# A gated feed-forward layer on one core: order of loads and stores between its first two stages

## The chip, the cores and the metric

The kernel runs on one core of one Trainium2 chip. The metric is device time in microseconds (us), from the start of the program to its end. The core has five engines with queues of their own, and 16 DMA engines that they share: TensorE (PE, matmuls; its weight loads are listed as PEld), VectorE (DVE), ScalarE (ACT), GpSimd (POOL) and SyncE (SP), which here issues the DMA transfers and nothing else.

## The reference

```python
def _gelu(x):
    return jax.nn.gelu(x, approximate=True)
...
B, S, Dm, Df = 1, 2048, 1024, 3584
...
def reference(x, w_gate, w_up, w_down):
    g = jnp.einsum("bsd,df->bsf", x, w_gate)
    u = jnp.einsum("bsd,df->bsf", x, w_up)
    h = _gelu(g) * u
    return jnp.einsum("bsf,fd->bsd", h, w_down)
```

All arrays are bfloat16.

## The kernel before

**Passes and stages.** The 2048 rows of x are taken in two passes (`ip`) of 1024 rows, each as two column blocks of 512. A pass has two stages. The first makes h: 14 *units* of 256 columns of `w_gate` and `w_up` each. The second, `down`, multiplies h with `w_down`, whose 28 blocks of 128 rows are taken as 14 *blocks* `j` in two halves `kh`.

**Fewer products.** Both stages use a seven-product scheme of 2 by 2 blocks instead of eight products. That needs sums of blocks, which are made in 32 bits: `s1` to `s4` of weights (mostly GpSimd, `pool`), `t1` to `t4` of x (DVE), and copies `sa`, `tb` (ACT). For the units 4 to 13 of the first pass (`pair0`, two units at a time) one of the seven products is itself split once more; its sums are `r1` to `r4`, and x's are kept in the tile `forms`. What the second pass needs again of it goes to device memory (`pd`).

**Differences of w_down.** The down stage's products use three differences of blocks of `w_down` for each `j`. They are made once, in the first pass, and stored to device memory (`td`) for both passes. For most blocks ACT and DVE make them between the products (`keep_part`, line 578 on). Blocks 12, 13 and 11 are made by GpSimd at the end of the first stage (`keep_whole`, three subtractions each). `BIGS` lists 1, 4, 12, 13, 11: blocks whose raw weights lie in a large tile of the pool `w`; `fetch_wd` loads them.

**The end of the first stage.** `last_of_0` is the last pair (units 12 and 13) of the first pass. In the order of its calls on SP: `hooks("made", 10)` stores the differences of block 10 and then loads four raw down tiles ahead (`fetch12(0)` to `fetch12(3)`; one such tile feeds two blocks j of one half kh); `hooks("wholes", 0)` loads block 11, has GpSimd make blocks 12, 13 and 11, and stores 12; `hooks("pd", 13)` stores one part of `pd`; `hooks("home", 13)` is `bring_home`, eight copies that gather parts of h, kept elsewhere until then, into the tile `hL`, which takes the place of `forms`; `hooks("pd", 12)`; and `hooks("wholes", 1)`, close to the end, stores 13.

**The down stage.** `down` runs over steps. Steps 0 to 13 multiply the first half's raw tiles with h, steps 14 to 27 the second half's: 4 matmuls each, so 8 for each raw tile. From step 28 on the second product uses the second differences (`q12`, reloaded from `td` by `load12`) and sums of h (`s12`, made by DVE in `make12`). From step 31 the first differences follow. From step 45 come `q73` and at last `q4` with `sa`. What is issued at a step is an agenda: `need12` fetches raw tile n at step 2n - 8 unless it was fetched ahead; `load12(j)` runs at step `AT12[j]`, where j = 0, 2, 4 load two blocks at once into a tile of the pool `w` (1 MB) and j = 6, 7 go to the pool `m`; `make12(j)` at `AT12S[j]`; `fetch73` and `make73` at `AT73[j] - 3` and `AT73[j]`. `more(step)` holds what the first pass does for the second beside that: the store of block 11 at step 2, x's next transposing loads from step 24, the next weights at step 50 and their sums at step 58.

**Order.** `manual_schedule` fixes the order of SP, DVE, GpSimd and PE as the code calls them (ACT's too in the first stage). So an SP transfer that must wait holds back all transfers behind it. The pools hand out buffers in the order in which they were given back: `k` has 36 slots of 2 KB per partition (raw tiles, x's sums, `u2`, `p5`, `g`, `q` and others), `s` has 13, `w` three, `m` two. A transfer into a slot waits until the slot's last readers are done.

The names in the profile: `raw<-in_w_down_dram` from L658 are the raw tiles of `fetch12`, from L641 those of `fetch73`; `w<-in_w_down_dram` and `raw<-in_w_down_dram` from L575 are `fetch_wd`; `td<-m` from L601 and L603 are the stores of differences; L950 is `pd`; L350 to L355 are `bring_home`; L613, L618 and L624 are `load12`; L634 is `load4`; L788 is x's transposing load; L144 loads `w_gate` and `w_up`. All matmuls of the stages go through L134, DVE's sums through L110, GpSimd's through L113.

Of the kernel before, what the change touches and what calls it, by code (L numbers as in the profile page):

```python
# [10 lines left out]
def kernel(  # L11
# [52 lines left out]
    BIGS = (1, 4, 12, 13, 11)  # L64
    LAG = 3
    BIG12 = (0, 2, 4)
    AT12 = [6, 6, 10, 10, 14, 14, 16, 18, 20, 22, 27, 29, 31, 33]
    AT12S = [2 * j + (j > 8) for j in range(NJ)]
    AT73 = [30 + 2 * j if j < 8 else 46 + j - 8 for j in range(NJ)]

# [391 lines left out]
    def last_of_0(a, roles, sa, sb, q, t, A, B, p5a, u2b, u2r, hooks):  # L462
        F, C, K, E = roles
        b = a + 1
        dve(F[1], F[1], p5a[1], SUB)
        part(E, q["r1"], T1, True)
        p5r = [snap(E[i], "p5", A[i]) for i in range(2)]
        part(K, q["r3"], T3, False)
        for i in range(2):
            dve(A[i], K[i], p5r[i], ADD)  # L470
        times(2 * a + 1, 0, gelu(F[0]), F[1])
        sb.make("sa")
        hooks("wholes", 0)
        part(E, q["r4"], TB, False)
        hooks("pd", b)
        part(K, [x[:, H:] for x in sb["s1"]], T4, False)
        hooks("home", b)
        for i in range(2):
            dve(B[i], E[i], u2r[i], ADD)
        hooks("pd", a)  # L480
        full(C, sb["s3"], t["t3"])
        p5b = [snap(K[i], "p5") for i in range(2)]
        full(K, sb["s4"], t["tb"])
        g, up = add(C, p5b)
        g = gelu(g)
        times(2 * b + 1, 1, g, up)
        full(C, sb["sa"], t["t4"])
        hooks("wholes", 1)
        hadd(K, u2b, 2 * b, 1)
        squared(C, p5b, 2 * b + 1)  # L490
        return roles
# [72 lines left out]

    def fetch_wd(js):
        for j in js:
            if j not in BIGS:
                wraw[j] = [slot([P, Dm], bf16, "raw") for _ in range(2)]
            else:
                n = BIGS.index(j) % 2  # L570
                if n == 0:
                    big = wpool.tile([P, 4, Dm], bf16, name="w")
                wraw[j] = [big[:, 2 * n + kh] for kh in range(2)]
            for kh in range(2):
                nc.sync.dma_start(out=wraw[j][kh], in_=wdn[:, kh, j, :])  # L575
# [303 lines left out]
    def upgraded(u):  # L879
        return FIRST <= u <= LAST  # L880
# [30 lines left out]
    for ip in range(NPASS):  # L911
        with tc.manual_schedule(engines={ENG.Activation}):
            if ip == 0:
                ws = {1: w, 2: ahead}
                late = lambda: add(cc, nxt["p1"])
            else:
                raw_of(0, F)()
                raw_of(1, C)()
            for u in range(1 if ip == 0 else 0, NU):
                if upgraded(u):  # L920
                    if u % 2:
                        continue
                    if u == FIRST:
                        S = {u: s, u + 1: sums_s(W(u + 1), pool)}
                    if (ip, u) == (0, FIRST):
                        fetch_wd(MID.values())
                        for n in range(4):
                            for c in range(2):
                                away[NH + n, c] = lambda n=n, c=c: staged(n, c)
                        away[NH + 4, 0] = lambda: hx  # L930

                    def hooks(what, n):
                        if what == "w":
                            if n < NU:
                                W(n)
                            if (ip, n) == (0, NU):
                                fetch_wd(BIGS[2:4])
                            if ip == 0 and n - 3 in JS:
                                fetch_wd(JS[n - 3][1:])
                            if ip == 0 and n - 2 == NH // 2 + 1:  # L940
                                send_out()
                            if ip == 0 and n - 3 == NH // 2 + 1:
                                move_on()
                            if ip and n <= LAST:
                                fetch_p5(n)
                        if what == "home" and n == LAST:
                            bring_home()
                        if what == "pd":
                            k = 0 if n % 2 else KH
                            nc.sync.dma_start(  # L950
                                out=pd[:, n - FIRST].rearrange("p i n -> p (i n)"),
                                in_=flat(xT[1][:, k : k + KH]),
                            )
                        if what == "made":
                            store_made(n)
                            if n == JS[LAST - 1][0]:
                                for m in range(4):
                                    fetch12(m)
                                    ahead12.add(m)
                        if what == "wholes" and n == 0:  # L960
                            fetch_wd(BIGS[4:])
                            for j in BIGS[2:]:
                                keep_whole(j)
                            store_made(BIGS[2])
                        if what == "wholes" and n == 1:
                            store_made(BIGS[3])
                        if what == "fetch":
                            fetch_wd(JS[n + 2][:1])

                    roles = F, C, K, E  # L970
                    if ip == 0:
                        F, C, K, E = pair0(u, roles, S, t, JS[u], hooks)
                    else:
                        F, C, K, E = pair1(u, roles, S, t, hooks)
                    continue
                first = (ip, u) == (0, 1)

                def prepare():
                    if first:
                        pool_behind(t["t4"][-1])  # L980
                    if ip == 0 and u in (2, 3):
                        lo_part(u - 2, 3, K)
                    if u + 1 < NU:
                        nxt["s"] = make_s(W(u + 1), pool, nxt.get("s"))
                    if (ip, u) == (0, FIRST - 2):
                        fetch_wd(JS[FIRST][:1])

                def keep(part, ps):
                    if ip == 0 and u in (2, 3):
                        for n in ((0, 1), (), (2,))[part]:  # L990
                            lo_part(u - 2, n, ps)

                def aside(part):
                    if first and part < 0:
                        rest_of_0(part + 2)
                    if part == 0 and u + 2 < NU:
                        W(u + 2)
                        if ip and upgraded(u + 2):
                            fetch_p5(u + 2)
                        if (ip, u) == (0, 1):  # L1000
                            load_lo()
                    if part == 0 and "t4" not in t:
                        t.make("t4")

                def ahead_of_p4():
                    if u % 2 and u + 1 < NU:
                        raw_of(u + 1, F)()
                        nxt["c11"] = raw_of(u + 2, C)

                def behind_p4():  # L1010
                    if "c11" in nxt:
                        nxt.pop("c11")()

                if u % 2 and not first:
                    E, K, C = C, E, K
                banks = (E, K, C) if u % 2 else (F, K, E)
                unit(
                    u, banks, s, t, late if first else None, prepare, aside, keep,
                    ahead_of_p4, behind_p4,
                )  # L1020
                s = nxt.pop("s", None)
# [4 lines left out]
        def more(step):  # L1026
            if last:
                return
            if step == 2:
                store_made(BIGS[4])  # L1030
            if step == 0:
                xT[:] = new_x()
            if step >= 24 and step % 2 == 0 and step // 2 - 12 < len(moves):
                c, ko = moves[step // 2 - 12]
                transposing(xT, c, ko, (2 * (ip + 1) + c) * N)
            if step == 50:
                ws.clear()
                ws.update({n: load_w(n) for n in range(2)})
            if step == 58:
                got["s"] = make_s(ws[0], dve)  # L1040
            if step == 62:
                got["t"] = make_t(xT)
# [34 lines left out]
```

## Time and profile before

| | us |
|---|---|
| median of three runs | 548.55 (546.86 to 548.73) |
| the profiled execution | 547.19 |
| its span | 545.4 |
| PE busy | 531.4 (97%) |
| DVE busy | 369.1 (68%) |
| ACT busy | 281.6 (52%) |
| POOL busy | 270.2 (50%) |
| first stage, first pass, to | 197.6 |
| down stage, first pass, to about | 296.6 |

The profiled execution lasts 1.8 us longer than its span, which runs from the first to the last instruction. The page gives first the busy time of each engine, then the span in 40 slices of 13.6 us with each engine's busy tenths, the granted clock of PE and the DMA engines' share; then the chain of work that ended last, by engine; then groups of instructions with their mean time and what ended the idle time before them. In a timeline, a line is the start and duration of a group of instructions of one kind, and in brackets the idle time before it and what ended that. SPq is SP's queue; its lines show how long SP took to issue a transfer, not how long that took. A line of a table of stretches gives for each engine its busy time and the number of instructions, then granted clock, DMA share and GB/s. In the whole execution the core moved 107.71 MB, 197 GB/s on average.

### The profile page before, as it was taken

The page shows a single profiled execution, that of the slowest core. Times are in us where ns is not written, and L with a number is a line of the kernel's source. Part 1 is how long each engine was busy: PE and PEld are TensorE (multiplying, and loading weights), DVE is VectorE, ACT ScalarE, POOL GpSimd, SP SyncE. Part 2 cuts the span into 40 slices and gives each one's busy share as a digit, 9 for nine tenths or more (in the row PEclk, how much of TensorE's full clock was granted, in tenths as well). Part 3 has the DMA queues.
Part 4 walks back from the last instruction along what each step waited for, and adds up shares of the span by engine and source line. Part 5 has one row for each costly group of instructions (what it writes and reads, how often), then busy time and mean ns, then how long its engine had stood idle before and what let it go on. Part 6 is the DMA issues. An engine that isn't in the chain of part 4 may idle for free.

```text
span 545.4 us, 7557 instructions
## 1 busy us (share of the span) xinstructions
PE 531.4 (97%) x2389; PEld 376.7 (69%) x2389; DVE 369.1 (68%) x573; ACT 281.6 (52%) x508; POOL 270.2 (50%) x258
## 2 busy tenths in 40 slices
PE   8999999999999994999999999999999999999997
PEld 4568686868686861378887768676686675488885
DVE  2989678787777794556877654665765859875830
ACT  3567686968686720104354555656566662104351
POOL 1089958879897940000003868896679740000000
PEclk9999999999999997999999999999999999999999
DMA  9795227676676879997894835233834439655571
GB/s 250 169 241 151 78 94 270 197 270 214 210 239 235 271 258 339 390 304 201 228 299 170 217 106 143 82 103 87 231 103 131 115 101 361 251 174 159 169 242 48
DMA packets 118407, 107.71 MB, mean 197 GB/s; under 512 B 22112, under 2 KB 98656, under 8 KB 118368
## 3 DMA queue, kind: packets, MB, share of 16 engines
q1 hardware_dynamic: 118368, 107.24, 64.7%
q8 instruction: 19, 0.31, 0.2%
q14 instruction: 20, 0.16, 0.1%
HBM read 80.22 MB, written 20.97 MB: 186 GB/s over the span
## 4 chain that ended last, share of the span: by engine, by line
PE 91%; DMA 4%; SPq 2%; DVE 2%; issue 0%; ACT 0%; DVEq 0%; ACTq 0%
PE bank L134 91%; DMA raw<-in_w_down_dram 2%; DMA w<-td 1%; DVE q L110 1%; DMA w<-in_w_up_dram 1%; SPq L601 1%; SPq L658 1%; DVE hL L110 0%; SPq L775 0%; DVE bank L110 0%; SPq L950 0%; SPq L618 0%; ACT g L202 0%; DVE sum L110 0%; ACT st L747 0%
## 5 line engine op out<-in xcount | busy, mean ns | idle before, releaser
L113 POOL TENSOR_TENSOR s<-w 128x512 fp32r<-128x512 bf16 x102 | 119.4, 1188 | 152.3 <-PE bank L134 106.1
L134 PE MATMUL bank<-t,s 128*128 128x512 f32 x528 | 126.1, 392 | 0.0
L134 PEld LDWEIGHTS bank<-t,s 128*128 128x128 f32 x528 | 99.1, 188 | 21.3
L134 PE MATMUL bank<-xT,w 128*128 128x512 bf16 (+1 forms) x504 | 110.4, 376 | 0.0
L134 PEld LDWEIGHTS <-w 128*128 128x128 bf16 x504 | 47.8, 98 | 58.3 <-issue 4.2
L127 ACT COPY p<-bank 128x512 f32<-128x512 f32 x98 | 55.7, 591 | 58.0 <-PE bank L134 58.0
L202 ACT ACTIVATE g<-sum 128x512 f32<-128x512 f32 x81 | 51.5, 636 | 62.5 <-DVE sum L110 60.2
L110 DVE TENSOR_TENSOR hT<-g,bank 128x512 bf16<-128x512 f32 x72 | 49.0, 687 | 16.6 <-ACT g L202 10.4
L110 DVE TENSOR_TENSOR sum<-bank,p 128x512 f32<-128x512 f32 x54 | 37.1, 686 | 32.9 <-PE bank L134 28.1
L113 POOL TENSOR_TENSOR s<-w,s 128x512 fp32r<-128x512 bf16 x50 | 57.8, 1173 | 0.4
L113 POOL TENSOR_TENSOR s<-s,w 128x512 fp32r<-128x512 f32 x50 | 57.5, 1167 | 0.5
L110 DVE TENSOR_TENSOR bank<-bank,p 128x512 f32<-128x512 f32 x74 | 51.3, 695 | 6.7 <-PE bank L134 6.5
L122 ACT CAST tb<-raw 128x512 fp32r<-128x512 bf16 x28 | 17.4, 628 | 74.2 <-PE bank L134 30.6
L134 PE MATMUL bank<-t,sa 128*128 128x512 f32 x216 | 54.9, 397 | 0.0
L134 PE MATMUL bank<-tb,s 128*128 128x512 f32 x216 | 54.2, 393 | 0.0
L134 PE MATMUL bank<-q 128*128 128x512 f32 x208 | 51.7, 389 | 0.0
L134 PEld LDWEIGHTS bank<-t,sa 128*128 128x128 f32 x216 | 40.6, 188 | 9.1
L134 PEld LDWEIGHTS bank<-tb,s 128*128 128x128 f32 x216 | 40.6, 188 | 8.7
L134 PEld LDWEIGHTS bank<-q 128*128 128x128 f32 x208 | 39.1, 188 | 8.1
L134 PE MATMUL bank<-raw,hT 128*128 128x512 bf16 x144 | 33.0, 390 | 8.1 <-DMA raw<-in_w_down_dram 8.1
L127 ACT COPY u<-bank 128x512 f32<-128x512 f32 x56 | 32.2, 596 | 13.9 <-PE bank L134 13.9
L134 PEld LDWEIGHTS <-hT 128*128 128x128 bf16 x144 | 14.3, 100 | 26.4 <-issue 10.8
(82 smaller groups left out, 664.2 us busy)
## 6 DMA issues: line engine op xcount, KB each, us to landing
raw<-in_w_down_dram SPq DMA_DIRECT2D x70, 256.0 KB, 4.7
w<-in_w_gate_dram SPq DMA_DIRECT2D x27, 512.0 KB, 4.3
w<-in_w_up_dram SPq DMA_DIRECT2D x27, 512.0 KB, 5.7
q<-td SPq DMA_DIRECT2D x52, 256.0 KB, 4.4
td<-m SPq DMA_DIRECT2D x11, 768.0 KB, 5.1
w<-td SPq DMA_DIRECT2D x6, 1024.0 KB, 10.0
pd<-xT SPq DMA_DIRECT2D x10, 512.0 KB, 5.9
p<-pd SPq DMA_DIRECT2D x20, 256.0 KB, 3.0
```

The source lines that it names most:

```text
L110: nc.vector.tensor_tensor(out=out, in0=a, in1=b, op=op)
L113: nc.gpsimd.tensor_tensor(out=out, in0=a, in1=b, op=op)
L122: nc.scalar.copy(out=t, in_=src)
L127: nc.scalar.copy(out=t, in_=ps)
L134: nc.tensor.matmul(ps, lhsT=lhs, rhs=rhs, start=start, stop=stop, skip_group_check=True)
L202: nc.scalar.activation(g, src, ACT.Gelu_apprx_tanh)
L601: nc.sync.dma_start(out=td[:, j, n], in_=made[j][n].bitcast(f32))
L658: nc.sync.dma_start(out=rl, in_=wdn[:, kh, j : j + 2, :N])
```

## The change

The raw weights of block 11 move out of the pool `w` into two tiles of the pool `k` (`BIGS[:4]` in `fetch_wd`). After the store of block 10, six raw down tiles are loaded in place of four, and block 11's two raw tiles right behind them; before, block 11 was loaded at `hooks("wholes", 0)`. The store of block 13 moves from `hooks("wholes", 1)` to step 5 of the down stage, that of block 11 from step 2 to step 9. `AT12`, the steps at which the differences are loaded back, becomes later for j = 0 to 11. No arithmetic changes.

```diff
-    AT12 = [6, 6, 10, 10, 14, 14, 16, 18, 20, 22, 27, 29, 31, 33]
+    AT12 = [12, 12, 15, 15, 18, 18, 20, 22, 24, 26, 28, 30, 31, 33]
...
         full(C, sb["sa"], t["t4"])
-        hooks("wholes", 1)
         hadd(K, u2b, 2 * b, 1)
...
     def fetch_wd(js):
         for j in js:
-            if j not in BIGS:
+            if j not in BIGS[:4]:
                 wraw[j] = [slot([P, Dm], bf16, "raw") for _ in range(2)]
...
                             if n == JS[LAST - 1][0]:
-                                for m in range(4):
+                                for m in range(6):
                                     fetch12(m)
                                     ahead12.add(m)
+                                fetch_wd(BIGS[4:])
                         if what == "wholes" and n == 0:
-                            fetch_wd(BIGS[4:])
                             for j in BIGS[2:]:
                                 keep_whole(j)
                             store_made(BIGS[2])
-                        if what == "wholes" and n == 1:
-                            store_made(BIGS[3])
...
-            if step == 2:
-                store_made(BIGS[4])
+            if step in (5, 9):
+                store_made(BIGS[3 + step // 8])
```

## The prediction

> **What bounds the kernel now.** I read the page from the top: TensorE (PE) is busy for 97% of the span and 91% of the chain that ended last, so a change is worth what it does to PE's idle time. The two rows of slices that matter here (40 slices of 13.6 us):
>
> ```profile
> PE   8999999999999994999999999999999999999997
> DMA  9795227676676879997894835233834439655571
> ```
>
> One slice is a hole: the sixteenth, 204.5 to 218.2 us, the start of the first pass's down stage. There the DMA engines are busy, and one slice earlier (8) they were not. PE's timeline shows what the hole costs:
>
> ```profile
> 197.60 7.08 PE L134 MATMUL bank<-raw,hT 128*128 128x512 bf16 x32
> 212.44 8.36 PE L134 MATMUL bank<-raw,hT 128*128 128x512 bf16 x32 [7.76 <-DMA raw<-in_w_down_dram]
> 221.11 1.89 PE L134 MATMUL bank<-raw,hT 128*128 128x512 bf16 x8 [0.31 <-DMA raw<-in_w_down_dram]
> ...
> 225.19 3.61 PE L134 MATMUL bank<-raw,hL 128*128 128x512 bf16 x16 [0.46 <-DMA raw<-in_w_down_dram]
> 229.23 3.91 PE L134 MATMUL bank<-raw,hL 128*128 128x512 bf16 x16 [0.43 <-DMA m<-td]
> 232.79 8.56 PE L134 MATMUL bank<-w,q 128*128 128x512 f32 x36
> ```
>
> Call the fourteen raw down loads R0 to R13; each feeds 8 matmuls. R0 to R3 were fetched ahead and their 32 matmuls take 7.08 us, 6.91 without the pipelined end, 1.73 per load. At that pace the q matmuls begin at 197.60 + 14 x 1.73 = 221.8; they begin at 232.79. **The stage loses 11.0 us**: 7.76 waiting for R4, 1.3 because 32 matmuls then take 8.36 instead of 7.08 (the granted clock in 210-215 was 0.50), the rest for later loads.
>
> Why R4 was late is on SP's queue. Its waits between 183 and 232 us, and its issues:
>
> ```profile
> SPq L575 <- POOL m L113: 6.6, 1, 6.6
> ...
> SPq L618 <- DMA w<-td: 2.7, 1, 2.7
> ```
>
> ```profile
> 186.00 0.48 SPq L658 DMA_DIRECT2D raw<-in_w_down_dram  x1
> 193.23 0.82 SPq L575 DMA_DIRECT2D w<-in_w_down_dram  x2
> ...
> 208.09 1.42 SPq L658 DMA_DIRECT2D raw<-in_w_down_dram  x2
> ```
>
> The second line: SP lets eight transfers be under way (the m load of 220.34 went out as the load issued eight before it, at 212.73, landed). The first is the hole's cause: SP issues R3 at 186.00 and then stands 6.6 us before block 11's loads, whose w buffer holds blocks 12 and 13 until GpSimd's differences (POOL m) end at 193.20. Behind that wait, in SP's order, stand the store of 12, the pd store of unit 13, the home copies, the pd store of 12, the store of 13, and only then R4 (208.09). The DMA engines show both sides:
>
> ```profile
> 190.80:195.60 4.80, 4.80 (x23) 3.97 (x23) 4.35 (x8) 2.89 (x6) 2.32 (x2) 1.00 0.28 70
> 195.60:212.50 16.90, 9.14 (x43) 4.68 (x42) 10.85 (x16) 1.12 (x2) 3.49 (x3) 0.87 0.94 340
> 212.50:231.25 18.75, 17.41 (x72) 7.29 (x72) 11.73 (x18) 2.05 (x4) 0.00 (x0) 0.93 1.04 382
> ```
>
> Last three numbers: clock, DMA share, GB/s. Almost 5 us of idle transfer time, then saturation until PE runs free.
>
> **The change, part by part.** Everything is on SP's queue; no compute instruction is added or removed.
>
> *Eight loads ahead of the stores.* R4 and R5 (0.65 us of issue each, the mean of R0 to R3) follow R3: SP reaches 187.8. Block 11's two (0.41 each) follow: 188.6. They now come from the pool k of 36 slots instead of w. Counted in the code at that point, 20 k tiles are live (t3, t4, tb four each, r1 to r4, two u2, two sa), so 16 slots are free and eight are taken; the next in turn were last read by 182 us (t1, t2, the keep casts, the last sums), so I charge no wait. Bounds: zero to the rival below. The 6.6 us wait is gone; GpSimd's differences of 11 start when 13's end, but nothing on the path waits for them.
>
> *What moves up behind them.* The store of 12 waits for its third difference (ends 189.57): 1.43 us, to 191.0. The pd store waits for DVE (191.41): 0.95, to 192.4. Home waits for PE's last read of forms (192.32); from its first issue to the end of the second pd store SP needed 205.55 - 196.66 = 8.9 us: to 201.3. Then R6 0.65, the store of 13 2.46 (now at step 5), R7 and R8 1.42, the store of 11 1.44 (step 9), R9 and R10 1.59, the load of q 0 and 1 0.52 (step 12), R11 0.47, q 2 and 3 0.75 (step 15), R12 0.66: 211.3. PE needs R6 at 197.60 + 6 x 1.73 = 208.0, and SP issued it by 202.0: SP isn't late any more, and eight issues before R12 lies a store of 11, landed near 211: no wait there either.
>
> *So the transfers decide.* From R4 through R12 the queue carries R4, R5 and 11 (1,024 KB), the store of 12 (768), pd (512), home (2,176), pd (512), R6 (256), store 13 (768), R7, R8 (512), store 11 (768), R9, R10 (512), q 0-1 (1,024), R11 (256), q 2-3 (1,024), R12 (256): 10,368 KB, 10.62 MB, starting where R3 landed (190.77). The rate isn't shown for this mix; the rows give 340 and 382 GB/s. I take the middle, 361 (the unbroken stretch 196.0-204.67 gave 354): 29.4 us, so **R12 lands at 220.2**. PE needs it at 218.3: 1.9 us late. By the same count R11 lands at 216.6, just when it is needed, R13 at 220.9 (needed 221.9), q 0-1 at 215.8. The q matmuls begin at 220.2 + 2 x 1.73 = 223.7 instead of 232.79: **9.1 us won**. At 382 GB/s R12 lands at 218.6 and 10.7 are won; at 340, at 222.0, and 7.3.
>
> The Trainium skill ("DMA: Bandwidth & Descriptors", Bandwidth) puts the limit of HBM per core at about 358 GB/s and the ports' at 435; the row of 382 lies between. By 358 R12 would land at 220.4 and 8.9 us be won: it speaks against the 10.7, not against the change.
>
> *A wait of 1.9 us and the clock.* The waits of 0.31 to 0.46 us left the clock at 1.00 in 220-230; the one of 7.76 halved it. Between those ends I charge nothing, being nearer to the short ones; the other end is 1.3 us.
>
> The skill ("TensorE: Matmul & The Clock Gate", Part 1) has the clock halved after an idle window of about 3.4 us, which by itself would leave 1.9 us unpunished; no run here shows a wait of that length.
>
> *Edits at zero.* The stores of 13 and 11 free pool s tiles for DVE: before, its make12 steps waited for them until 209.31 and 213.90 and ended at 226.0. By the count above 11's first store lands near 210; 18 sums of 0.67 end near 222.4, before the four output sums at 223.7. Those take 2.48 us and PE reuses their banks 3.9 us after its first q matmul, so DVE may be 1.4 us late before PE waits. Pool s has 13 tiles and 7 free at step 0: make12 takes six before step 5 gives three back, and three more come at step 9. *Reloads of q later:* the last of the w-sized ones (q 4-5) follows R13 and lands at 223.7, needed at 228.2; q 8 lands about 227.6, needed at 235.5. From block 13 on SP waits for slots that PE frees (245.91 before), so what SP lags behind PE ends there.
>
> **The sum** goes against the profiled execution's own 547.19 us (span 545.4 and 1.8 around it): 547.19 - 9.1 = 538.1. The median shown, 548.55, lies 1.36 above, so I give 539.4.
>
> **Rivals.** *Supply is worse, or part is given back.* At 340 GB/s 7.3 are won; with the halved clock 6.0: 542.5. The end of the pass has the same sign: DVE's sums of next w (277.0 on, after a wait of 1.0 for its load) precede the sums that free e's banks, the last done at 283.72, and PE needs that bank at 284.5: loads that lag PE by over 0.8 us more cost the excess one to one. For it: DMA share 0.98 in 233-260. Against: SP waited 2.4 and 1.5 us for PE at 244-248, slack that takes up a lag of 2 us. 20%: 540.5 to 543.5.
> *Nothing stands in the way*: 382 GB/s or more, and all 11.0 but 0.3 come back: 537.8. Against: the row of 340 is the one with stores in it. 13%.
> *The loads block the queue.* If fewer than eight slots are free at the hook, SP stands there with every store and the home copies behind it, and next slot comes from PE's reads of R0, over at 199.5 us. R4 would then land no sooner than 203.8 (R3 took 4.3 from the end of its issue), 12.3 later than behind R3; R12 about 232.4, the q matmuls 235.9, 3.1 later than before: 551.7. It decides from the ninth live tile above my 20, and costs more than it brings once SP stands beyond 196.4. Against: the count, and R0 to R3, which waited 0.4 and 0.6 us in all. 7%.
> *It doesn't do what it says*: the wait for 11 goes but the hole merely moves to R6 to R13, within 0.5% of 548.55. The saturated 382 GB/s speaks for it; the 5 idle us that are filled and the 1.5 MB (q 4-5, m 6) that now follow R13 speak against. 5%.
> Forecast as summed, 7.3 to 10.7 won: 55%, its own range 537.8 to 541.3.
>
> **How the numbers follow.** Time 539.4. The range takes the forecast, the first rival to its end and the lower end of the runs shown (546.86 - 10.7 = 536.2): 536.3 to 543.5. A measurement tells about 0.5% (2.7 us) from no change; all of forecast, worse supply and full gain lie beyond it: faster 0.88, within 0.05, slower 0.07.
>
> **What would show it.** SP without the wait for POOL m, block 11 landed near 193; DMA share above 0.9 in 190-196; PE's first wait in the down stage at R11 or R12, under 3 us, at full clock; first q matmul near 223.7; from there on the trace of before, 9 us earlier. Wrong it is if SP stands at the hook, if a wait appears at q 8 to q 13 or at 275 (DVE for w), or if the hole stays over 6 us.

## The result, and the profile after

Eleven runs of each: before 547.15 us (546.48 to 549.07), after **542.71 us** (541.42 to 547.23), a ratio of 0.9913 (95%: 0.989 to 0.9936); one run of after took 547.23, the other ten 544.33 or less. The change made the kernel faster by 4.4 us, about half of the 9.1 that were predicted. The profiled execution of after has a span of 539.6 us (before 545.4), so 5.8 of the sum's 9.1.

The slices of the page of after:

```profile
PE   9999999999999979999999999999999999999997
DMA  9795218685767699999994744441744439465571
```

The hole in the sixteenth slice (4) is gone. There is a smaller one, a 7, one slice earlier (188.9 to 202.4 us), where PE had run at 9 before. The DMA engines no longer pause there. The table of stretches (busy time and instructions of PE, PEld, DVE, ACT and POOL, then clock, DMA share, GB/s) shows that transfers now run without a break:

```profile
190.00:196.00 6.00, 4.71 (x21) 3.40 (x19) 3.08 (x5) 2.08 (x4) 3.97 (x5) 1.00 1.03 355
196.00:212.00 16.00, 13.99 (x58) 8.01 (x59) 12.27 (x19) 3.34 (x6) 3.05 (x3) 0.89 1.06 400
212.00:226.00 14.00, 14.00 (x67) 6.32 (x66) 11.05 (x17) 2.05 (x4) 0.00 (x0) 1.00 1.11 382
```

The same three stretches of before had shares of 0.31, 0.94 and 1.04. SP's timeline shows the new order: block 11's two loads and the store of block 12 go out by 191.2. (Line numbers shift a little from kernel to kernel: `fetch12` is L658 in before, L657 here, L661 in e1.)

```profile
184.46 3.66 SPq L657 DMA_DIRECT2D raw<-in_w_down_dram  x6
188.17 0.93 SPq L574 DMA_DIRECT2D raw<-in_w_down_dram  x2
189.28 1.92 SPq L600 DMA_DIRECT2D td<-m  x3
```

Of SP's waits for GpSimd (6.6 us in before, at block 11's loads) the list of waits has 0.4 us left, at the store of block 12:

```profile
SPq L600 <- POOL m L113: 0.4, 1, 0.4
```

PE's timeline has what was won and what was lost:

```profile
192.72 2.00 PE L134 MATMUL bank<-t,s 128*128 128x512 f32 x8
198.01 3.39 PE L134 MATMUL bank<-tb,s 128*128 128x512 f32 x8 [3.30 <-POOL m L113]
201.23 1.98 PE L134 MATMUL bank<-t,sa 128*128 128x512 f32 x8
203.06 15.71 PE L134 MATMUL bank<-raw,hT 128*128 128x512 bf16 x72
218.61 8.80 PE L134 MATMUL bank<-raw,hL 128*128 128x512 bf16 x40
227.06 8.54 PE L134 MATMUL bank<-w,q 128*128 128x512 f32 x36
```

The 112 matmuls of the down stage's raw tiles now run from 203.06 to 227.06 without one wait: 24.0 us where before took 35.2. But a wait stands ahead of them that before had not: 3.30 us before the product tb,s of the last pair, in the first stage. Its eight matmuls then take 3.39 us; the eight of t,s just before took 2.00.

Three marks of PE's timeline, and the span, divide the time of each kernel (us from the start of the span; R0 here is the first matmul of the down stage). The first mark is this line, of before and then of after:

```profile
185.76 1.07 PE L134 MATMUL bank<-forms,r 128*128 128x512 f32 x4
```

```profile
186.33 1.07 PE L134 MATMUL bank<-forms,r 128*128 128x512 f32 x4
```

| kernel | first product with r, last pair | R0 | first q matmul | span | pair to R0 | R0 to q | q to end |
|---|---|---|---|---|---|---|---|
| before | 185.76 | 197.60 | 232.79 | 545.4 | 11.84 | 35.19 | 312.6 |
| after | 186.33 | 203.06 | 227.06 | 539.6 | 16.73 | 24.00 | 312.5 |
| after, block 11 in pool m (e1) | 186.30 | 198.13 | 223.12 | 535.7 | 11.83 | 24.99 | 312.6 |

The stage that the prediction is about gives 11.2 us; the last pair takes 4.9 back, and 0.6 was lost before the pair, nearly all of it by 25 us (the first products `t,s` of the program start at 23.91 in before and 24.44 in after): 5.7. Behind the first q matmul nothing is won or lost.

Who made PE wait stands on ACT and POOL. ACT's timeline of after, then POOL's:

```profile
191.49 0.63 ACT L122 CAST sa<-w 128x512 fp32r<-128x512 bf16 x1
196.76 0.62 ACT L122 CAST sa<-w 128x512 fp32r<-128x512 bf16 x1 [4.65 <-POOL m L113]
197.28 1.06 ACT L127 COPY p<-bank 128x512 f32<-128x512 f32 x2
```

```profile
191.27 2.43 POOL L113 TENSOR_TENSOR m<-w,m 128x512 fp32r<-128x512 bf16 x2
195.58 1.15 POOL L113 TENSOR_TENSOR m<-raw 128x512 fp32r<-128x512 bf16 x1 [1.88 <-DMA td<-m]
196.81 2.40 POOL L113 TENSOR_TENSOR m<-raw,m 128x512 fp32r<-128x512 bf16 x2
```

ACT's second cast of `sa` reads nothing that GpSimd writes. It starts 0.03 us after GpSimd's first difference of block 11 ends (196.73). My reading is that it needs the slot: `sa` comes from pool k, and the slot that it is handed is one of block 11's raw tiles, which that difference reads. DVE's first sum of unit 13, also a tile of pool k, fits the same reading: it started right after the end (199.2) of GpSimd's third difference, the last reader of block 11's other tile. PE didn't wait for it.

```profile
199.24 0.69 DVE L110 TENSOR_TENSOR sum<-bank,p 128x512 f32<-128x512 f32 x1 [5.49 <-POOL m L113]
```

Behind the cast on ACT stand the two `p5` copies that read the banks K, and PE's product tb,s writes those banks. GpSimd in turn had waited 1.88 us for a buffer of `s` that the store of block 12 had to empty. The chain of waits (start, duration, what) runs through all of it:

```profile
184.46 4.76 DMA raw<-in_w_down_dram
...
189.28 6.17 DMA td<-m
...
195.58 0.57 POOL m L113
...
196.81 1.17 POOL m L113
...
198.01 338.16 PE bank L134 x1504
```

The first part of that store took 6.17 us from issue to landing, behind eight loads; in before, behind two, it took 3.6. In one place the names want care: profile and chain put PE's wait down to GpSimd's second difference, which ended at 197.98. PE's product doesn't use it. PE's queue passed its two semaphores at 197.9 and 198.4, when the first and the second `p5` copy ended (197.86 and 198.34); the second difference only ended near them. e3 below has the same wait with the copy named.

### The profile page after: what moved, and what is told of

Its sections match the earlier page's. It is cut to its first block, busy times and chain, and to the rows that moved or that the text cites. A ratio compares the mean times of both kernels' runs of the same rounds, so it can differ in the third digit from the quotient of the medians.

```text
span 539.6 us, 7564 instructions
## 1 busy us (share of the span) xinstructions
PE 531.9 (99%) x2389; PEld 378.2 (70%) x2389; DVE 367.6 (68%) x573; ACT 282.0 (52%) x508; POOL 271.1 (50%) x258
## 4 chain that ended last, share of the span: by engine, by line
PE 94%; DMA 3%; ACT 1%; issue 0%; SPq 0%; DVE 0%; POOL 0%; POOLq 0%; DVEq 0%
PE bank L134 94%; DMA td<-m 1%; DMA raw<-in_w_down_dram 1%; DMA w<-in_w_up_dram 1%; ACT bank L583 0%; POOL m L113 0%; SPq L774 0%; DVE m L110 0%; ACT u L127 0%; ACT p L127 0%; ACT xT L127 0%; DVE sum L110 0%; ACT st L746 0%; SPq L793 0%; ACT g L202 0%
## 5 line engine op out<-in xcount | busy, mean ns | idle before, releaser
L134 PE MATMUL bank<-tb,s 128*128 128x512 f32 x216 | 55.6, 401 | 3.3 <-POOL m L113 3.3
L122 ACT CAST sa<-w 128x512 fp32r<-128x512 bf16 x54 | 30.7, 617 | 4.6 <-POOL m L113 4.6
L110 DVE TENSOR_TENSOR q<-raw 128x512 fp32r<-128x512 bf16 x28 | 19.3, 688 | 19.3 <-DMA raw<-in_w_down_dram 13.5
```

What stands on the lines that cost most here:

```text
L110: nc.vector.tensor_tensor(out=out, in0=a, in1=b, op=op)
L122: nc.scalar.copy(out=t, in_=src)
L134: nc.tensor.matmul(ps, lhsT=lhs, rhs=rhs, start=start, stop=stop, skip_group_check=True)
```

## Experiments

Theory, from this reading: what is lost in the pair is the price of block 11's two tiles being in pool k, because ACT is handed one of them next; the rest of the prediction's mechanism holds. The main rivals: the six raw tiles and the later stores carry the gain and block 11's place matters little; or GpSimd is merely late, whatever slot it reads.

### e1: block 11 out of pool k

After, with block 11's raw weights in a free tile of pool `m`, loaded at the same place in SP's order:

```
-                wraw[j] = [slot([P, Dm], bf16, "raw") for _ in range(2)]
+                if j == BIGS[4]:
+                    two = mpool.tile([P, 2, Dm], bf16, name="raw11", tag="m")
+                    wraw[j] = [two[:, kh] for kh in range(2)]
+                else:
+                    wraw[j] = [slot([P, Dm], bf16, "raw") for _ in range(2)]
```

> The changed kernel, but block 11's raw weights take a free tile of pool m instead of two slots of pool k. Theory (slot coupling: ACT's second sa copy of unit 13 takes the k slot of block 11's raw weights and so waits for GpSimd's difference of block 11; PE stands behind ACT): that wait of ACT (4.65 us) and PE's wait of 3.3 us before the tb,s4 product vanish, the down stage starts near 198.1 instead of 203.06, R12 lands near 219.7 as in the changed kernel and becomes the bound by about 1 us, first q matmul near 223.3 instead of 227.06, span 535.2 to 536.5, ratio to before about 0.982. Rival (the denser transfers or the fuller pool k hold ACT back, wherever block 11 lies): a wait of 2 us or more stays in the last pair and the time is within 1 us of the changed kernel's.

Measured: 537.78 us against 547.95 before, **0.9813 (0.9798 to 0.9828)**. ACT's timeline, then PE's:

```profile
191.18 1.15 ACT L122 CAST sa<-w 128x512 fp32r<-128x512 bf16 x2
192.47 1.08 ACT L127 COPY p<-bank 128x512 f32<-128x512 f32 x2
```

```profile
194.50 1.98 PE L134 MATMUL bank<-tb,s 128*128 128x512 f32 x8
...
198.13 15.71 PE L134 MATMUL bank<-raw,hT 128*128 128x512 bf16 x72
...
219.86 3.61 PE L134 MATMUL bank<-raw,hL 128*128 128x512 bf16 x16 [0.83 <-DMA raw<-in_w_down_dram]
223.12 8.54 PE L134 MATMUL bank<-w,q 128*128 128x512 f32 x36
```

GpSimd's first difference of block 11:

```profile
194.15 1.18 POOL L113 TENSOR_TENSOR m<-raw 128x512 fp32r<-128x512 bf16 x1 [0.52 <-DMA raw<-in_w_down_dram]
```

The casts run back to back, although this difference ended only at 195.33, 3.6 us after the second cast started. So the wait came from the slot. GpSimd is 1.4 us earlier than in after too, since its first difference no longer waits for the store; that can't be why the cast is free, for the cast is over before the difference begins. The pair takes 11.83 us, as before. The only wait left in the down stage is the one that the prediction had: for R12, 0.83 us, at full clock.

### e2: after without block 11's move

```
-            if j not in BIGS[:4]:
+            if j not in BIGS:
...
-                                fetch_wd(BIGS[4:])
...
+                            fetch_wd(BIGS[4:])
```

> The changed kernel, but block 11 is loaded where and into what it was before (pool w, behind GpSimd's differences of 13). Theory (slot coupling): no wait of ACT or PE in the last pair; SP's wait for GpSimd of some 6 us is back; R6 is late and R12 lands near 224, first q matmul 227 to 228, so 5 to 6.5 us faster than before, about like the changed kernel. Rival (denser transfers or two more raw tiles in pool k hold ACT back): PE's wait in the last pair stays at 2 us or more and the ratio is above 0.994.

Measured: 542.9 us, 0.991 (0.9893 to 0.9927). Nothing waits in the pair (R0 11.85 us after the first product with r), but SP waits 5.4 us for GpSimd and the DMA share in 190 to 196 is 0.56. PE pays in the down stage, most of it at R6, and again at R12:

```profile
211.79 2.42 PE L134 MATMUL bank<-raw,hT 128*128 128x512 bf16 x8 [2.71 <-DMA raw<-in_w_down_dram]
...
226.48 3.61 PE L134 MATMUL bank<-raw,hL 128*128 128x512 bf16 x16 [1.44 <-DMA raw<-in_w_down_dram]
```

Waits of 5.0 us in four places, and a clock of 0.88 in 212 to 226; the first q matmul comes at 229.74, some two us later than I expected. The 24 matmuls behind the wait at R6 took 1.5 us more than at full clock, but that isn't what came last: R12 landed at 226.44, where I had put it near 224, and PE stood 1.44 us for it. e2 and after take the same time for different reasons: what SP's wait for POOL costs in the down stage is about what the pair loses when block 11 goes into pool k.

### e3: block 11's move alone

Before, with only `fetch_wd(BIGS[4:])` moved behind the four raw tiles, and into pool k:

```
-            if j not in BIGS:
+            if j not in BIGS[:4]:
...
                                 for m in range(4):
                                     fetch12(m)
                                     ahead12.add(m)
+                                fetch_wd(BIGS[4:])
                         if what == "wholes" and n == 0:
-                            fetch_wd(BIGS[4:])
```

> The kernel before, with block 11's loads alone moved: into pool k, behind four raw tiles. Theory (slot coupling): the wait in the last pair appears here too (the second p5 copy of unit 13 now takes the slot), 2 to 5 us of ACT; R4 then comes some 4 us earlier than before, R12 by byte count near 223.7, first q matmul near 227, so 5 to 6.5 us faster than before: the wait is hidden behind the transfers. Rival (the six raw tiles and later stores carry the gain): ratio above 0.996.

Measured: 541.95 us, 0.9893 (0.9878 to 0.9907): as much as the whole change. The rival that the six raw tiles and later stores carry the gain falls in the form that I gave it (nothing won without them). But e2 has these edits without block 11's move, and wins as much: each part alone gives 5 to 6 us, and together, with the pair's wait gone (e1), they give 10. ACT's timeline, then PE's:

```profile
195.76 0.58 ACT L127 COPY p<-bank 128x512 f32<-128x512 f32 x1 [2.30 <-POOL m L113]
```

```profile
196.40 1.20 PE L134 MATMUL bank<-tb,s 128*128 128x512 f32 x4 [0.41 <-ACT p L127]
...
208.00 7.07 PE L134 MATMUL bank<-raw,hT 128*128 128x512 bf16 x32 [1.64 <-DMA raw<-in_w_down_dram]
```

Two fewer raw tiles are fetched here, and the slot of block 11's first tile goes to ACT's second copy of `p5`, two requests further on than the second `sa`. The wait is for the end of the same difference (195.72) and PE loses 0.41 us to it instead of 3.30. How much a slot costs depends on whose turn it is. In the down stage 4.3 us of waits are left, and the first q matmul comes at 228.34, 1.3 later than expected.

### e9: GpSimd later, slots as they are

After, with GpSimd computing the last difference of block 13 five times over (the same values), four extra subtractions of 1.25 us ahead of block 11:

```
-        pool(m[2], rb[:, :N], m[1], SUB)
+        for _ in range(5 if j == BIGS[3] else 1):
+            pool(m[2], rb[:, :N], m[1], SUB)
```

> The changed kernel with more work: GpSimd computes the last difference of block 13 five times instead of once (four times 1.17 us or more, the same values), so block 11's differences come some 3 us later or more. Theory (slot coupling): with that, the order in which slots are given back shifts in the program, ACT's second sa copy takes the slot of a gelu long done, and a gelu of unit 13, which PE doesn't wait for, takes block 11's; so PE's wait in the last pair (3.3 us) vanishes although GpSimd is later, and the time is that of e1_11_in_m within 1 us, ratio 0.980 to 0.984. Rival (GpSimd is simply too slow for the new order, or the transfers hold it back): the wait grows by some 3 us, ratio 0.995 or more.

Measured: 542.47 us against 547.38, 0.9906 (0.9891 to 0.9921), no different from after. Both expectations miss a part. GpSimd started its first difference 2.7 us later (198.31), yet ACT's casts and `p5` copies didn't wait at all: by this reading the slots were handed out in another order. ACT's timeline, then PE's:

```profile
191.10 1.15 ACT L122 CAST sa<-w 128x512 fp32r<-128x512 bf16 x2
192.13 1.10 ACT L127 COPY p<-bank 128x512 f32<-128x512 f32 x2
199.50 0.63 ACT L202 ACTIVATE g<-sum 128x512 f32<-128x512 f32 x1 [6.27 <-POOL m L113]
```

```profile
200.90 1.19 PE L134 MATMUL bank<-t,sa 128*128 128x512 f32 x4 [3.84 <-DVE hL L110]
```

Now the gelu of unit 13 seems to hold the slot: it starts 0.04 us after GpSimd's first difference ends (199.46). I had written that PE would not wait for it; it did, 3.84 us, since the product t,sa writes a bank that DVE's multiplication with that gelu reads. So the time of a late GpSimd doesn't add up simply; it passes through whoever holds the slot. That the order of handing out is fixed by what the build takes the times to be would explain it, and no run shows that.

### e4, e5, e6, e8: the other parts, with the pair's wait gone

All four are e1 with one thing changed. e4 ran beside e1; the others ran later, beside before at 547.38 us, so they are compared with e1 by their ratios.

e4, the reloads' steps of before:

```
-    AT12 = [12, 12, 15, 15, 18, 18, 20, 22, 24, 26, 28, 30, 31, 33]
+    AT12 = [6, 6, 10, 10, 14, 14, 16, 18, 20, 22, 27, 29, 31, 33]
```

> As e1_11_in_m, but the differences are loaded back at the steps of before. If transfers bound the down stage once the pair's wait is gone: 1 MB more ahead of R12, which lands near 223.7, first q matmul near 227, 3 to 4 us slower than e1_11_in_m. If the later reloads are worth nothing: within 0.7 us of e1_11_in_m.

Measured: 540.6 us, 0.9862 (0.9845 to 0.9878). Five waits for raw tiles, 3.2 us in all (time, number, longest), the first q matmul at 226.39, 3.3 later than e1.

```profile
PE bank L134 <- DMA raw<-in_w_down_dram: 3.2, 5, 1.4
```

The later reloads are worth about 3 us.

e5, the stores of 13 and 11 where before had them:

```
+        hooks("wholes", 1)
...
+                        if what == "wholes" and n == 1:
+                            store_made(BIGS[3])
...
-            if step in (5, 9):
-                store_made(BIGS[3 + step // 8])
+            if step == 2:
+                store_made(BIGS[4])
```

> As e1_11_in_m, but 13 is stored at the end of the last pair and 11 at step 2, as before. If what counts is the bytes ahead of R12 alone: R6 lands near 209.4 instead of 205.4, 0.9 us late, R12 where it was, first q matmul 223.1 to 223.6, time within 0.8 us of e1_11_in_m. If a late R6 costs more (a chain of waits, the halved clock): 1.5 us or more slower.

Measured: 538.03 us against 547.38, 0.9829 (0.9814 to 0.9844). R6 is waited for 1.60 us (I had 0.9), but then R12 isn't, and the first q matmul is 0.8 later than in e1.

```profile
210.29 5.34 PE L134 MATMUL bank<-raw,hT 128*128 128x512 bf16 x23 [1.60 <-DMA raw<-in_w_down_dram]
```

The later stores are worth under 1 us; the intervals of e1 and e5 overlap.

e6, four raw tiles ahead:

```
-                                for m in range(6):
+                                for m in range(4):
```

> As e1_11_in_m, but four raw tiles ahead instead of six. By byte count R4 lands near 205.4, needed at 205.0, R12 where it was (219.8): within 0.8 us of e1_11_in_m. If six ahead are needed: 1.5 us or more slower, with a wait of over 1.5 us at R4.

Measured: 539.67 us, 0.985 (0.9827 to 0.9873): 2 us slower than e1, where a count of bytes had promised the same within 0.8. The transfers are the same, in another order; the rate isn't. The same stretch in e1, then in e6:

```profile
204.00:208.00 4.00, 4.00 (x20) 1.83 (x19) 1.99 (x4) 0.00 (x0) 0.00 (x0) 1.00 1.06 391
```

```profile
204.00:208.00 4.00, 4.00 (x20) 1.79 (x19) 1.23 (x3) 0.00 (x0) 0.00 (x0) 1.00 0.98 342
```

From 200 to 216 e6 moved 342 to 360 GB/s and e1 388 to 411, at DMA shares of 0.98 to 1.03 and 1.04 to 1.07. R12 landed at 221.35 instead of 219.81, and PE waits 0.99 and 1.45 us where e1 waits 0.83; what else is lost lies at the end of the pass (next paragraphs). Why the rate is lower isn't settled; that other kinds of transfer lie beside each other in those us is all that the trace shows.

e8, reloads later still:

```
-    AT12 = [12, 12, 15, 15, 18, 18, 20, 22, 24, 26, 28, 30, 31, 33]
+    AT12 = [12, 12, 17, 17, 19, 19, 20, 22, 24, 26, 28, 30, 31, 33]
```

> As e1_11_in_m, with the reloads of q 2-3 and q 4-5 at steps 17 and 19 instead of 15 and 18, so behind R12 and R13. R12 lands near 217.2 and R13 near 220.5, needed at 218.8 and 220.6: no wait left in the down stage, first q matmul near 222.3 instead of 223.12, span 534.7 to 535.3. If the reloads become late instead: a wait at q 2 or q 4, span 536 or more.

Measured: 536.94 us, 0.9811 (0.979 to 0.9832). No wait for a transfer is left in the down stage and the first q matmul comes at 222.16, 0.96 before e1; the span is only 0.3 shorter. The rest is given back at the end of the pass. The waits between 260 and 292 us (in all, times, longest), e1's first, then e8's:

```profile
DVE s L110 <- DMA w<-in_w_gate_dram: 2.9, 1, 2.9
```

```profile
DVE s L110 <- DMA w<-in_w_gate_dram: 4.5, 1, 4.5
...
PEld bank L134 <- DVE st L110: 0.8, 2, 0.4
```

DVE stands before its sums of the next weights until their load lands, the sums that free the banks `e` follow late, and PE's weight loads wait for them. e6 has the same two lines (5.1 and 1.2 us). In e1 and in after DVE waits too (2.9 and 3.8 us), but PE doesn't wait for DVE.

## Why the prediction was half right

**What held.** *What bounds the kernel:* the hole belonged to the queue order and not to the rate; filled, it gave all of its 11 us. (In the DMA row of before the slice ahead of the hole reads 7, not 8; nothing rests on it.) *SP's wait goes:* of 6.6 us for POOL m, 0.4 is left on SP, at the store of 12; block 11 landed at 194.09 and 194.77 ("near 193"), the DMA share in 190 to 196 is 1.03 ("above 0.9"). *The transfers decide, at R12:* it landed at 219.69 in after and 219.81 in e1 (predicted 220.2). In e1, where PE comes in time, R12 is the only wait, 0.83 us (predicted 1.9) at full clock, and the first q matmul comes at 223.12 (predicted 223.7). Two errors of the count nearly cancel there. The rate was higher than my 361: 355, 400 and 382 GB/s in the three stretches shown, so by 219.7 us some 5.2 x 355 + 16 x 400 + 7.7 x 382 = 11.2 MB had moved since 190.8. And not all of that is in the count of 10.62 MB: the rest of R3, which landed at 191.42, and transfers that SP issued behind R12 (R13, and more from 211.13 on) shared the engines with it. The Trainium skill's limit of about 358 GB/s for HBM ("DMA: Bandwidth & Descriptors", Bandwidth) would have R12 land at 220.4, by the prediction's working; the mix of this queue, with copies inside the core in it, ran above that rate. *The edits at zero:* DVE's sums for the second product ended at 223.42 in after, ahead of the need; nothing waited at q 8 to q 13.

**The step that failed** is in the first edit: "*Eight loads ahead of the stores.* ... 20 k tiles are live ..., so 16 slots are free and eight are taken; the next in turn were last read by 182 us ..., so I charge no wait." It is right for the loads: SP stood at most 0.6 us at any of the raw loads, as it did at R0 to R3 in before, and the rival of the blocked queue didn't come. But I only asked whether the loads find slots. I didn't ask **who is given block 11's slots back next, and when**. The step's last sentence closes the question with the same error: "GpSimd's differences of 11 start when 13's end, but nothing on the path waits for them." Before, block 11 lay in the pool `w`, so nothing of ACT's stood behind those differences. In pool k the next owner is ACT's second cast, directly ahead of the copies that free PE's banks. Cost: 4.65 us on ACT; on PE 3.30 and then 1.4 in the eight slow matmuls that follow; 4.9 in the pair as a whole. A second miss lies in the same sentence: the differences of 11 did not start when 13's ended (193.70) but at 195.58, because the store of 12, which frees GpSimd's output buffer, now queues behind eight loads on the DMA engines. The prediction counted SP's time for that store, and not its 6.17 us to landing.

**The terms together.** Predicted: 9.1 us won. Measured on the spans: 11.2 in the down stage (no wait at R12 either, PE being 4.9 us later, so 1.9 of the charge was hidden), less 4.9 in the pair, less 0.6 before it, 5.7. With the failed step mended and nothing else (e1) the span is 9.7 shorter. The time, 542.71, fell inside the range (536.3 to 543.5), and luck helped: the forecast starts from a median of three runs, 548.55, which with eleven runs is 547.15. From there the sum gives 538.0, and the miss is 4.7 us and not the 3.3 that 539.4 suggests. The time lies in the interval of the first rival, "supply is worse, or part is given back", but not for its reason: supply was better than forecast, and in after nothing was given back at the end of the pass. That rival's second mechanism is real; e6 and e8 show it, once PE leads the loads by more.

**The clock.** The wait of 3.30 us in after was followed by eight matmuls in 3.39 us instead of 2.00 and a granted clock of 0.89 in 196 to 212, the one of 2.71 in e2 by eight in 2.42 us instead of 1.89 and 0.88 in 212 to 226, the one of 3.84 in e9 by a clock of 0.89 in 196 to 212. Waits of 1.64 (e3), 1.60 (e5) and 0.83 (e1) left it at full. A row of e2, then one of e3:

```profile
212.00:216.00 4.00, 3.82 (x12) 1.21 (x11) 2.27 (x4) 2.05 (x4) 0.00 (x0) 0.63 0.95 336
```

```profile
196.00:212.00 16.00, 13.96 (x63) 7.15 (x64) 13.65 (x21) 1.99 (x4) 2.14 (x2) 1.00 1.02 370
```

In e2 the clock fell late: it was still 1.00 in 212 to 213, with PE back at work since 211.79, and 0.50 in 213 to 216. My choice of nothing for a wait of 1.9 us is at least not contradicted. The idle window of about 3.4 us that the Trainium skill states ("TensorE: Matmul & The Clock Gate", Part 1) isn't a safe line here: both 3.30 and 2.71 us lie below it, and both were followed by a lower clock.

## What to carry to other kernels

A load that is moved ahead takes a buffer, and hands it on only when its reader is done: besides asking whether the load finds a slot, follow the slot to its next owner, and from there along that engine's queue to the path. A tile that a slow side engine reads late is better kept out of a pool that the engines on the path draw from (here a spare tile of `m`: 0.9813 instead of 0.9913). When the releaser that a profile names writes nothing that the waiting instruction reads, look for a shared buffer.

## What the runs showed of the hardware that was not expected

- Transfers that never pause moved 397 to 400 GB/s over 16 us (196 to 212 in e1 and after). From 200 to 216 e1 moved 388 to 411 GB/s, and e6, with the same transfers in another order and a DMA share of about 1 as well, 342 to 360. A share of 1.0 doesn't mean that the rate can't rise.
- A wait of PE of 2.71 us was followed by a lower granted clock (e2), one of 1.64 us wasn't (e3). In e2 the clock fell only some 1.2 us after PE was back at work.
- The first part of the store of 12 took 6.17 us from issue to landing behind eight loads (after) and 5.9 behind six (e3); behind two it took 3.6 (before) and 3.5 (e2).
